# Loads of a turn released nine matmuls later, and one addition moved ahead of another in a two-layer kernel after retention

## The chip, the cores and the metric

The kernel runs on one core of a Trainium2 chip. The metric is the time of one execution on the device, in microseconds (us). The core has a matrix engine (PE, with its weight loads shown apart as PEld), a vector engine (DVE), a scalar engine (ACT), a general engine (POOL), and SP, which here issues nearly all DMAs. Each engine goes through its own list of instructions in order, and waits for others by semaphores.

## The reference

Eight batches, eight heads, 576 positions, head size 64. First retention, a causal attention without softmax whose scores decay by head; then a layer to 2048 and back to 512, with `h - tanh(h)` between:

```
scores = scale * np.matmul(q, k.transpose(0, 1, 3, 2))
gamma = 1.0 - 2.0 ** (-5.0 - np.arange(H))
Dmat = np.where(rel >= 0, gamma[:, None, None] ** rel[None, :, :], 0.0)
ret = np.matmul(scores * Dmat[None], v)          # (B, H, S, D)

x = ret.transpose(0, 2, 1, 3).reshape(B * S, H * D)   # 4608 x 512
h = x @ w_in                                     # 4608 x 2048
g = h - np.tanh(h)
out = g @ w_out                                  # 4608 x 512
```

## The kernel before, in words

**Tiling.** The 576 positions are cut into nine chunks of 64 (`n` or `c`, 0 to 8). A chunk of all eight batches is 512 tokens. The layer of 2048 is cut into 16 slices of 128 (`f`). Retention is done in chunks: a pair of batches (a *turn*, `m`) needs a tile of q and k (`qk`, 512 KB), a tile of v and k by rows (`vr`, 512 KB), and a running `state`. Matmuls take fp32 numbers split into a high and a low word, so a product of the two layers is three matmuls.

**Stages.** From chunk 2 on the program alternates between two kinds of stage. `stage_b(n)` does the second layer of chunk n and, beside it, retention of later chunks. Then `stage_a(na)` does the first layer of two chunks at once (na and na + 1), and the second layer of chunk na. The order is b(2), a(3), b(4), a(5), b(6), a(7), b(8).

**stage_b.** It has 16 steps, one for each slice f. An even step begins with `attend(m)`, the retention of one pair of batches: on PE 128 small matmuls (64x64 on quarters of the array). Each step has the 12 matmuls of `mm2(n, f)`; they need the two words of h of this slice (`gh` and `gl`, or `gs`), which `split` made two steps earlier out of a tile `s` that `fetch` brought back from DRAM (256 KB, it had been spilled there), four steps ahead. An even and the odd step after it make a turn. In the even step the program then issues `load_turn(..., 0, ...)`, the `qk` tile of three turns on, and the fetch of slice f + 4; in the odd step `load_turn(..., 1, ...)`, the `vr` tile of two turns on, and the next fetch. All four are on SP, in this order, and each `load_turn` is held back by `behind(tc, late)`: it waits until a named matmul of the step's own `mm2` is done (`names[2]` in even steps, `names[6]` in odd ones, counted from 0). What SP has behind it waits too.

In b(2) SP also gets the weights of the next stage (`ws`, `load_slot`: the first slot in quarters in steps 10 to 13, two slots of 1 MB in steps 14 and 15), the table of `work`, and at its end eight stores of the output (`out`, from the tiles `ob`).

**stage_a.** The first layer of two slices (a *pair* j of slices) by two chunks is done with seven products instead of eight (`product(0)` to `product(6)`, six matmuls each), whose results are combined on DVE: `u2` and `u4` are partial sums in the tile `work`, and `c22`, `c12`, x and `c21` are the four blocks of h. ACT and POOL or DVE make `h - tanh(h)` of them; `c22` and `c12` are spilled to DRAM for the next stage_b, the other two are split (`split`) and used at once by `mm2_pair`. In PSUM the products have five banks: x in `new` (for the first pair `o0`), y in `own`, z and v in two banks `h` that take turns. The work of the last block (`rest`: tanh, subtract, split of c21) follows directly in every pair but the first; the first pair's is put off into the second pair, ahead of `product(3)` and `c22`, by the list `pending`.

**What sets the order.** The order on every engine is the order in which the program is written (`in_order`); a tile's buffer is waited for where it is written next.

Of the kernel before, what the change touches and what calls it, by code (L numbers as in the profile page):

```python
# [14 lines left out]
ALU = mybir.AluOpType  # L15
# [50 lines left out]
def behind(tc, name):  # L66

    tc.add_manual_dep(
        tc.nc.cur_bb.bb.instructions[-1], name,
        mybir.DependencyInfo(mybir.DependencyClass.Sync, mybir.DependencyReason.DATA), reason="paced",  # L70
    )
# [3 lines left out]
def retention_ffn(ctx: ExitStack, tc: tile.TileContext, ins, out, spill, wvar):  # L75
    nc = tc.nc
# [120 lines left out]
    def load_qtab(c):  # L197
        if c not in qtabs:
            if c == 1:
                qtabs[c] = const.tile([P, 4, C], F32, tag="wo6", name="qtab1")  # L200
            else:
                qtabs[c] = pool.tile([P, 4, C], F32, tag="qtab", bufs=1, name=f"qtab{c}")
            nc.sync.dma_start(qtabs[c], qtab_d[c - 1])
# [495 lines left out]
    def place_of(f):  # L699
        return place("i", f) if f != 1 else "wi14"  # L700
# [85 lines left out]
    def load_turn(m, t, late=None):  # L786
        if m >= len(turns):
            return
        j = turns[m]
        c, b = divmod(j, B)  # L790
        if m == 1 and t == 0:
            load_qtab(c)
        if t == 0 and m and m % 8 == 0:
            tables.append(c)
        if t == 0 and m % 3 == 2:
            part = const.tile([P, 2, 2, 4, C], F32, tag=place_of(0), name=f"qk{j}")
        elif t == 0:
            part = pool.tile([P, 2, 2, 4, C], F32, tag="qk", bufs=2, name=f"qk{j}")
        else:
            part = pool.tile([P, 2, 2, 4, C], F32, tag=("vr", "one")[m % 2], bufs=1, name=f"vr{j}")  # L800
        nc.sync.dma_start(part, qkv_d[c - 1, ORDER[c].index(b) // 2, t])
        if late is not None:
            behind(tc, late)
        parts[j, t] = part
        for u in range(2):
            loaded.setdefault(j + u, Parts([None, None])).parts[t] = part[:, u]
# [92 lines left out]
    def load_slot(n, part=None):  # L899

        if n >= per * ((NC - FIRST) // 2):
            return
        if n not in slots:
            slots[n] = pool.tile([P, 4, 2, 2, P], F32R, tag=("xh0", "xh1", "xl0")[n % 3], bufs=1, name=f"ws{n}")
        at = slice(0, 4) if part is None else slice(part, part + 1)
        to = slots[n].bitcast(F32).rearrange("p v s c m -> p v (s c m)")[:, at]
        nc.sync.dma_start(to, wvar[:, 4 * (n % per) + at.start : 4 * (n % per) + at.stop])
# [3 lines left out]
    def product(v, into, start=True):  # L911

        n, at = divmod(count[0], 4)
        w, (xh, xl) = slots[n][:, at], xv[v]
        terms = [(a, x, k) for a, x in ((0, xh), (0, xl), (1, xh)) for k in range(2)]
        for i, (a, x, k) in enumerate(terms):
            nc.tensor.matmul(  # L917
                into, w[:, a, k], x[:, k], start=start and i == 0, stop=i == len(terms) - 1, skip_group_check=not start,
            )
        count[0] += 1  # L920
        if at == 3:
            load_slot(n + 3)

    def split(n, f, g, spare):

        if spare:
            both = const.tile([P, 2, BLK], F32R, tag=place_of(2), name="gs")
            gh, gl = both[:, 0], both[:, 1]
        else:
            gh = pool.tile([P, BLK], F32R, tag="gh", name=f"gh{n}_{f}")  # L930
            gl = pool.tile([P, BLK], F32R, tag="gl", name=f"gl{n}_{f}")
        nc.scalar.copy(gh, g)  # L932
        nc.vector.tensor_tensor(gl, g, gh.bitcast(F32), op=ALU.subtract)  # L933
        gs[n, f] = (gh, gl)

    def mm2_pair(n, j):

        if j == 0:
            ops[n] = [psp.tile([P, DM], F32, tag=f"o{t}", bufs=1, name=f"o{n}_{t}") for t in range(4)]
        fs, end = (2 * j + 1, 2 * j), j == NPAIR - 1  # L940
        if end:
            order = [(f, t, k) for t in range(4) for f in fs for k in range(3)]
        else:
            order = [(f, t, k) for f in fs for k in range(3) for t in range(4)]
        for f, t, k in order:
            g, a = [(gs[n, f][0], 0), (gs[n, f][0], 1), (gs[n, f][1], 0)][k]
            last_ = end and f == fs[1] and k == 2
            nc.tensor.matmul(  # L948
                ops[n][t], g[:, t * P : (t + 1) * P], wout[f][:, a, :],
                start=(j == 0 and f == fs[0] and k == 0), stop=last_,  # L950
            )
            if last_:
                store(n, t)

    def stage_a(na):

        nb, pending = na + 1, []
        u2, u4 = work[:, 0], work[:, 1]
        for j in range(NPAIR):
            x, y = [psp.tile([P, BLK], F32, tag=t, bufs=1, name=f"p{t}{na}_{j}") for t in ("new" if j else "o0", "own")]  # L960
            z, v = [psp.tile([P, BLK], F32, tag="h", bufs=2, name=f"p{t}{na}_{j}") for t in "zv"]
            f1, f2 = 2 * j, 2 * j + 1
            c22, c12, c21 = [pool.tile([P, BLK], F32, tag="g", bufs=3, name=f"c{t}_{na}_{j}") for t in (22, 12, 21)]

            def tanh(c):
                th = pool.tile([P, BLK], F32, tag="cv", bufs=4, name=f"th{na}_{j}")
                nc.scalar.activation(th, c, AF.Tanh)  # L967
                return th

            def away(c, f):  # L970
                nc.gpsimd.tensor_tensor(c, c, tanh(c), op=ALU.subtract)  # L971
                nc.sync.dma_start(spill[nb, f], c)

            product(0, x)
            product(1, y)
            nc.scalar.copy(u2, x)
            nc.vector.tensor_tensor(u2, y, u2, op=ALU.add)  # L977
            product(2, z)
            nc.vector.tensor_tensor(u4, z, u2, op=ALU.add)
            while pending:  # L980
                pending.pop()()
            product(3, v)
            nc.vector.tensor_tensor(c22, v, u4, op=ALU.add)  # L983
            y = psp.tile([P, BLK], F32, tag="own", bufs=1, name=f"py{na}_{j}")
            product(4, y)
            away(c22, f2)
            nc.vector.tensor_tensor(c12, y, u4, op=ALU.add)
            product(5, x, False)
            away(c12, f1)
            g11 = tanh(x)  # L990
            nc.vector.tensor_tensor(g11, x, g11, op=ALU.subtract)
            product(6, v, False)
            split(na, f1, g11, False)
            nc.vector.tensor_tensor(c21, v, u2, op=ALU.add)

            def rest(f=f2, c=c21, tanh=tanh):
                nc.vector.tensor_tensor(c, c, tanh(c), op=ALU.subtract)
                split(na, f, c, True)

            if j == 0:  # L1000
                pending.append(rest)
            else:
                mm2_pair(na, j - 1)
                rest()
        for f in range(3):
            fetch(nb, f)
        mm2_pair(na, NPAIR - 1)
        for f in range(2):
            split(nb, f, fetched.pop((nb, f)), False)
# [5 lines left out]
    def stage_b(n, m0):  # L1015

        fetch(n, 3)
        for f in range(NF):
            def ahead():
                if f + 2 < NF:  # L1020
                    split(n, f + 2, fetched.pop((n, f + 2)), f % 3 == 0)

            if n == 2 and f == 1:
                load_tables(FIRST)
            m, odd = m0 + f // 2, f % 2 == 1
            if n < NC - 1 and not odd:
                attend(m, ahead)
            else:
                ahead()
            if n == NC - 1:  # L1030
                fetch_on(n, f + 4)
            if n == 2 and f == NF - 1:
                load_slot(2)
            if (n, f) != (NC - 1, NF - 2):
                names = mm2(n, f)
            if n < NC - 1:
                load_turn(m + 3 - odd, int(odd), names[6 if odd else 2])
                fetch_on(n, f + 4)
            if odd and tables:
                load_tables(tables.pop())  # L1040
                set_tables()
            if n == 2 and f == 2:
                set_tables()
            if n == 2 and 9 < f < 15:
                load_slot(*((0, f - 10) if f < 14 else (1,)))
# [23 lines left out]
    work = pool.tile([P, 4, DM], F32, tag="xl1", bufs=1, name="work")  # L1069
# [63 lines left out]
```

## Time and profile before

| | |
|---|---|
| time, median of 3 | 859.01 us (855.62 to 859.25) |
| the profiled execution | 856.53 us, its span 854.8 us |
| PE busy in the span | 843.2 us (99%) |
| DVE, ACT, POOL busy | 484.6, 364.4, 74.3 us |
| DMA | 174.67 MB, 204 GB/s over the span |
| granted TensorE clock | 1.000 |

The span is the time from the first to the last instruction; some 1.7 us lie around it. PE is busy nearly all the time, so only the short stretches in which it waits are worth anything to a change that leaves PE's own work alone. The first 20 us and the last 5 us (start and end of the program) hold most of them.

### The profile page before, as it was taken

The numbers are of one execution on the slowest core, as the hardware profiler recorded it, in microseconds if no ns is written. First come the engines' busy times: TensorE is split into PE (matmuls) and PEld (weight loads), VectorE is DVE, ScalarE is ACT, GpSimd is POOL, SyncE is SP. The second block draws the span as 40 slices with busy tenths as digits, with TensorE's granted clock in tenths as the row PEclk, the third lists the DMA queues.
The fourth block names the chain that finished last, engine by engine and source line by source line (L and its number), as shares of the span: only waits on it lengthen the run. The fifth ranks groups of instructions, "written<-read, shape, count | busy, mean of one in ns | idle before, by whom it ended". The sixth has DMA issues, their size and how long they took to land.

```text
span 854.8 us, 18569 instructions
## 1 busy us (share of the span) xinstructions
PE 843.2 (99%) x7701; PEld 695.2 (81%) x7702; DVE 484.6 (57%) x817; ACT 364.4 (43%) x723; POOL 74.3 (9%) x63
## 2 busy tenths in 40 slices
PE   7999999999999999999999999999999999999998
PEld 6888888887888787888888788888888888888886
DVE  5989877868567665434346754434456554343321
ACT  4887774444234553323244443322345433232321
POOL 0001001110000001212110002211100012121100
PEclk9999999999999999999999999999999999999999
DMA  9976968776777579435376665534666255352432
GB/s 340 364 244 205 365 222 277 239 235 202 234 259 289 188 252 326 163 130 190 123 235 213 205 184 199 182 132 173 208 207 215 90 184 185 128 192 74 138 109 74
DMA packets 62404, 174.67 MB, mean 204 GB/s; under 512 B 7536, under 2 KB 8944, under 8 KB 57072
## 3 DMA queue, kind: packets, MB, share of 16 engines
q1 hardware_dynamic: 61792, 172.57, 59.5%
q8 instruction: 60, 0.98, 0.5%
q10 hardware_dynamic: 528, 0.92, 0.3%
q14 instruction: 24, 0.20, 0.1%
HBM read 124.70 MB, written 48.76 MB: 203 GB/s over the span
## 4 chain that ended last, share of the span: by engine, by line
PE 87%; issue 4%; DMA 4%; DVE 2%; ACT 1%; SPq 0%; POOL 0%; DVEq 0%; POOLq 0%; ACTq 0%
PE o L503 25%; PE o L948 15%; PE h L447 15%; PE pv L917 7%; PE pnew L917 6%; PE py L917 4%; PE pz L917 4%; PE pown L917 4%; PE s L300 3%; DMA s<-spill_dram 2%; PE new L300 2%; PE own L300 2%; DMA a<-in_first_dram 1%; PE po L917 1%; DMA rwi<-in_w_in_dram 1%
## 5 line engine op out<-in xcount | busy, mean ns | idle before, releaser
L503 PE MATMUL o<-wo,gh 128*128 128x512 f32 x608 | 156.8, 395 | 0.3 <-ACT gh L484 0.3
L503 PEld LDWEIGHTS o<-wo,gh 128*128 128x128 f32 x608 | 111.8, 188 | 26.8 <-ACT gh L484 2.2
L971 POOL TENSOR_TENSOR c<-c,th 128x512 f32<-128x512 f32 x48 | 62.0, 1297 | 516.6 <-ACT th L967 515.5
L967 ACT ACTIVATE th<-c 128x512 f32<-128x512 f32 x72 | 45.5, 632 | 140.9 <-DVE c L983 89.7
L447 PE MATMUL h<-xh,wi 128*128 128x512 f32 x384 | 97.7, 392 | 0.8 <-ACT xh L326 0.5
L447 PEld LDWEIGHTS h<-xh,wi 128*128 128x128 f32 x384 | 71.3, 188 | 16.9 <-ACT wi L129 0.8
L503 PE MATMUL o<-wo,gl 128*128 128x512 f32 x304 | 84.2, 389 | 0.0
L948 PE MATMUL o<-wo,gs 128*128 128x512 f32 x288 | 70.7, 389 | 0.0
L503 PEld LDWEIGHTS o<-wo,gl 128*128 128x128 f32 x304 | 57.1, 188 | 11.9
L948 PEld LDWEIGHTS o<-wo,gs 128*128 128x128 f32 x288 | 54.1, 188 | 11.2
L917 PE MATMUL pv<-xhv,ws 128*128 128x512 f32 x192 | 59.2, 390 | 0.6 <-DVE c L983 0.6
L503 PE MATMUL o<-wo,gs 128*128 128x512 f32 x240 | 59.2, 394 | 0.0
L300 PE MATMUL own<-qk,state 64*64 64x64 f32 x928 | 57.1, 221 | 0.0
L300 PE MATMUL own<-qk,vr 64*64 64x64 f32 x928 | 56.1, 218 | 0.7 <-issue 0.7
L977 DVE TENSOR_TENSOR work<-pown,work 128x512 f32<-128x512 f32 x24 | 16.6, 692 | 67.8 <-PE pown L917 67.1
L503 PEld LDWEIGHTS o<-wo,gs 128*128 128x128 f32 x240 | 44.4, 188 | 9.5
L917 PE MATMUL pnew<-xhv,ws 128*128 128x512 f32 x168 | 51.7, 389 | 0.0
L447 PE MATMUL h<-xl,wi 128*128 128x512 f32 x192 | 51.6, 389 | 0.0
L948 PE MATMUL o<-wo,gh 128*128 128x512 f32 x192 | 48.9, 389 | 0.0
L300 PEld LDWEIGHTS own<-qk,vr 64*64 64x64 f32 x928 | 46.6, 135 | 0.1
L300 PEld LDWEIGHTS own<-qk,state 64*64 64x64 f32 x928 | 46.2, 134 | 0.4 <-issue 0.4
L933 DVE TENSOR_TENSOR gl<-s,gh 128x512 fp32r<-128x512 f32 x44 | 30.0, 688 | 23.9 <-ACT gh L932 12.1
(152 smaller groups left out, 1516.4 us busy)
## 6 DMA issues: line engine op xcount, KB each, us to landing
ws<-wvar_dram SPq DMA_DIRECT2D x41, 1024.0 KB, 4.7
s<-spill_dram SPq DMA_DIRECT2D x94, 256.0 KB, 3.8
qk<-in_qkv_dram SPq DMA_DIRECT2D x29, 512.0 KB, 4.2
vr<-in_qkv_dram SPq DMA_DIRECT2D x29, 512.0 KB, 3.9
spill_dram<-c SPq DMA_DIRECT2D x48, 256.0 KB, 2.3
spill_dram<-g SPq DMA_DIRECT2D x36, 256.0 KB, 3.5
rwi<-in_w_in_dram SPq DMA_DIRECT2D x16, 512.0 KB, 5.6
rwo<-in_w_out_dram SPq DMA_DIRECT2D x16, 512.0 KB, 5.5
```

Source lines behind the costliest of these rows:

```text
L300: nc.tensor.matmul(out_, w, x, start=start, stop=stop)
L447: nc.tensor.matmul(hp, win[f][:, cc // 2, a, cc % 2 * P : (cc % 2 + 1) * P], x[:, cc, :], start=(k == 0), stop=(k == 3 * NCC - 1))
L503: nc.tensor.matmul(ops[n][t], g[:, t * P : (t + 1) * P], wout[f_][:, a, :], start=(f_ == first and k == 0), stop=(f_ == final and k == 2),)
L917: nc.tensor.matmul(into, w[:, a, k], x[:, k], start=start and i == 0, stop=i == len(terms) - 1, skip_group_check=not start,)
L933: nc.vector.tensor_tensor(gl, g, gh.bitcast(F32), op=ALU.subtract)
L948: nc.tensor.matmul(ops[n][t], g[:, t * P : (t + 1) * P], wout[f][:, a, :], start=(j == 0 and f == fs[0] and k == 0), stop=last_,)
L967: nc.scalar.activation(th, c, AF.Tanh)
L971: nc.gpsimd.tensor_tensor(c, c, tanh(c), op=ALU.subtract)
L977: nc.vector.tensor_tensor(u2, y, u2, op=ALU.add)
```

## The change

Three things. (1) In even steps of stage_b the `qk` load waits for the last matmul of the step (`names[11]`) and no longer for the third (`names[2]`); the fetch of h behind it on SP comes later with it. (2) In stage_a, `product(3)` and `c22` are written ahead of the put-off rest of the first pair. This matters in the second pair alone, where the list is not empty. (3) `u2` takes turns between two quarters of `work` (0 and 3), where it had one.

```diff
     def stage_a(na):
 
         nb, pending = na + 1, []
-        u2, u4 = work[:, 0], work[:, 1]
+        u4 = work[:, 1]
         for j in range(NPAIR):
+            u2 = work[:, 3 * (j % 2)]
...
             product(2, z)
             nc.vector.tensor_tensor(u4, z, u2, op=ALU.add)
+            product(3, v)
+            nc.vector.tensor_tensor(c22, v, u4, op=ALU.add)
             while pending:
                 pending.pop()()
-            product(3, v)
-            nc.vector.tensor_tensor(c22, v, u4, op=ALU.add)
             y = psp.tile([P, BLK], F32, tag="own", bufs=1, name=f"py{na}_{j}")
             product(4, y)
             away(c22, f2)
@@ stage_b
             if n < NC - 1:
-                load_turn(m + 3 - odd, int(odd), names[6 if odd else 2])
+                load_turn(m + 3 - odd, int(odd), names[6 if odd else 11])
                 fetch_on(n, f + 4)
```

**On DVE**, in the first stage_a (na = 3), from the last sum of the first pair (`c_3_0_4089` is its c21, `pv_1` and `py_1` are products of the second pair, `c_3_1_4160` its c22, `c_3_1_4161` its c12). Before:

```order
L994 TENSOR_TENSOR c_3_0_4089<-pv_0_4086,work 128x512 [waits PE_49]
L977 TENSOR_TENSOR work<-pown_1_4157,work 128x512 [waits PE_49,Activation_49]
L979 TENSOR_TENSOR work<-pz_1_4158,work 128x512 [waits DVE_49,PE_49]
L997 TENSOR_TENSOR c_3_0_4089<-c_3_0_4089,th_1_4186 128x512 [waits Activation_49]
L933 TENSOR_TENSOR gs<-c_3_0_4089,gs 128x512 [waits Activation_49]
L983 TENSOR_TENSOR c_3_1_4160<-pv_1_4159,work 128x512 [waits DVE_49,PE_49]
L987 TENSOR_TENSOR c_3_1_4161<-py_1_4199,work 128x512 [waits DMAHW5_49,PE_49,Pool_49]
```

With the change:

```order
L995 TENSOR_TENSOR c_3_0_4089<-pv_0_4086,work 128x512 [waits PE_49]
L978 TENSOR_TENSOR work<-pown_1_4157,work 128x512 [waits PE_49,Activation_49]
L980 TENSOR_TENSOR work<-pz_1_4158,work 128x512 [waits DVE_49,PE_49]
L982 TENSOR_TENSOR c_3_1_4160<-pv_1_4159,work 128x512 [waits DVE_49,DMAHW5_49,PE_49,Pool_49]
L998 TENSOR_TENSOR c_3_0_4089<-c_3_0_4089,th_1_4193 128x512 [waits Activation_49]
L933 TENSOR_TENSOR gs<-c_3_0_4089,gs 128x512 [waits Activation_49]
L988 TENSOR_TENSOR c_3_1_4161<-py_1_4199,work 128x512 [waits DMAHW6_49,PE_49,Pool_49]
```

The addition for c22 has moved ahead of two operations of the first pair, and it has new waits: it now takes the buffer of the first pair's c22, so it waits for POOL and for the store of that tile (`DMAHW5`), for which c12 waited before.

**On ACT**, in the same place. Before, and then with the change:

```order
L932 CAST gh_0_4151<-th_0_4142 128x512 [waits DVE_49]
L976 COPY work<-pnew_1_4156 128x512 [waits DVE_49,PE_49]
L967 ACTIVATE th_1_4186<-c_3_0_4089 128x512 [waits Pool_49]
L932 CAST gs<-c_3_0_4089 128x512 [waits DVE_49]
L967 ACTIVATE th_1_4208<-c_3_1_4160 128x512 [waits DMAHW7_49,DMAHW0_49,DVE_49]
```

```order
L932 CAST gh_0_4151<-th_0_4142 128x512 [waits DVE_49]
L977 COPY work<-pnew_1_4156 128x512 [waits PE_49]
L968 ACTIVATE th_1_4193<-c_3_0_4089 128x512 [waits DVE_49,Pool_49]
L932 CAST gs<-c_3_0_4089 128x512 [waits DVE_49]
L968 ACTIVATE th_1_4208<-c_3_1_4160 128x512 [waits DMAHW7_49,DMAHW0_49]
```

The order is as it was; the copy that begins u2 no longer waits for DVE, which is done with the last u2 only after c21.

**On SP**, at the end of b(2), where the rows read alike before and with the change (`qk_4047` is the load of step 14, the two `ws` behind it the 1 MB slots, `ob_0` the first tile of output, `vr_4081` the load of step 15, `c_3_0_4087` the first pair's c22):

```order
L801 DMA qk_4047<-in_qkv_dram 128x1024 [waits DMAHW0_49,DVE_49,PE_49]
L907 DMA ws_4049<-wvar_dram 128x2048 [waits DMAHW1_49]
L907 DMA ws_4051<-wvar_dram 128x2048 [waits DMAHW2_49]
L527 DMA out_dram<-ob_0_4056 64x512 [waits DMAHW3_49,Activation_49]
L527 DMA out_dram<-ob_0_4056 64x512 [waits DMAHW4_49]
...
L801 DMA vr_4081<-in_qkv_dram 128x1024 [waits DMAHW3_49,PE_49]
L907 DMA ws_4117<-wvar_dram 128x2048 [waits DMAHW4_49,PE_49]
```

Nothing moves in this list; the count of PE for which the first row waits is the one that lies nine matmuls later, and all that stands behind the row waits with it.

## The prediction

> **What bounds the kernel now.** I began with the page's first part, and then asked the busy times of the stages that the change touches (stretch, its length, busy us and count of PE, PEld, DVE, ACT, POOL; clock; DMA share; GB/s):
>
> ```profile
> PE 843.2 (99%) x7701; PEld 695.2 (81%) x7702; DVE 484.6 (57%) x817; ACT 364.4 (43%) x723; POOL 74.3 (9%) x63
> 262.00:303.00 41.00, 40.51 (x783) 33.53 (x772) 26.72 (x54) 20.17 (x53) 0.00 (x0) 1.00 0.65 227
> 303.00:341.00 38.00, 37.45 (x401) 30.61 (x400) 23.46 (x45) 16.07 (x39) 2.59 (x2) 1.00 0.86 294
> 443.00:506.00 63.00, 62.32 (x1221) 51.89 (x1221) 42.81 (x87) 31.89 (x85) 0.00 (x0) 1.00 0.62 198
> ```
>
> PE is the bound. Its holes are 0.49 us in b(2), 0.55 around the first stage_a, 0.68 in b(4). The change adds no matmul and takes none away, so it can win these holes and little more. Where they are is told by the chain of work that ended last (start, length, what): the 24 second-layer matmuls of a turn in b(2), b(4) and b(6), and a batch of 24 in stage_a.
>
> ```profile
> 277.58 5.67 PE o L503 x24
> 285.28 5.67 PE o L503 x24
> 293.69 4.55 PE o L503 x19
> 357.33 5.44 PE o L948 x24
> 475.81 5.67 PE o L503 x24
> 484.41 5.66 PE o L503 x24
> 634.86 5.67 PE o L503 x24
> 642.78 5.66 PE o L503 x24
> ```
>
> A turn takes 285.28 - 277.58 = 7.70 us. Three turns take longer: 293.69 - 285.28 = 8.41, 484.41 - 475.81 = 8.60, 642.78 - 634.86 = 7.92. Above 7.70 that is 0.71 + 0.90 + 0.22 = 1.83 us, one loss in each stage_b. PE's timeline shows the first two (in brackets the idle time and what ended it):
>
> ```profile
> 293.11 0.27 PE L300 MATMUL new<-vr 64*64 64x64 f32 x2 [0.49 <-issue]
> 483.94 0.21 PE L300 MATMUL own<-qk,vr 64*64 64x64 f32 x1 [0.68 <-issue]
> ```
>
> They lie inside `attend`, and no engine and no load ended them ("issue"). A turn has 152 matmuls (128 and 24) and as many weight loads, 304 instructions, and 256 of them pass in attend, in 7.70 - 5.67 = 2.03 us. So I looked for the queue of the instructions, q8, among the DMA queues (packets, MB, share). From 284.2 to 290.4 us and from 475.2 to 481.4 it moved nothing, while the loads' queue moved this:
>
> ```profile
> q1 hardware_dynamic: 510, 1.30, 60.9%
> q1 hardware_dynamic: 470, 1.15, 56.2%
> ```
>
> From 290.4 to 290.6 us its packet then started (the other one from 481.4 to 481.6):
>
> ```profile
> q8 instruction: 1, 0.02, 38.4%
> ```
>
> SP's issues of that turn, and the time in which its qk landed:
>
> ```profile
> 286.20 0.33 SPq L801 DMA_DIRECT2D qk<-in_qkv_dram  x1
> 289.84 0.33 SPq L801 DMA_DIRECT2D vr<-in_qkv_dram  x1
> qk<-in_qkv_dram SPq DMA_DIRECT2D x1, 512.0 KB, 3.5
> ```
>
> The packet started 0.7 us after qk had landed (286.20 + 3.5 = 289.7), and PE stood until 293.11. So these stops are, as I read them, PE without instructions, because the packet with them stood behind a burst of qk and h.
>
> The hole near 340 is another matter, and the chain tells it:
>
> ```profile
> 334.99 0.69 DVE c L994
> 335.76 0.59 ACT work L976
> 337.18 0.69 DVE work L979
> 339.15 0.70 DVE gs L933
> 339.95 0.70 DVE c L983
> 340.69 1.66 PE pv L917 x6
> ```
>
> PE's seventh product of the second pair (pv) waits for c22 (L983). On DVE that stands behind the put-off rest (which ends with L933), and u2's copy (L976) stands behind c21 (L994).
>
> **The change part by part.** *c22 and u2 (parts 2 and 3).* A matmul takes 5.44/24 = 0.227 us, a product of six 1.36. The pair's fourth product began at 335.87 (row below), so the seventh was due three products later, at 339.95, and began at 340.69; the hole costs 0.74. With c22 ahead of the rest, it needs only u4 (L979, ends at 337.87) and its product (335.87 + 1.36 = 337.23), and ends at 338.6, in time. Gain: 0.74. Late next is the rest, by the 0.7 us of one addition; its `gs` is used in the second half of the 24 matmuls that follow, 12 x 0.227 = 2.7 us behind the seventh product, which covers it; without that cover it would cost the 0.7. The new wait of c22, for the store of the first pair's c22, is the bound on the other side:
>
> ```profile
> 331.84 2.36 SPq L972 DMA_DIRECT2D spill_dram<-c  x2
> spill_dram<-c SPq DMA_DIRECT2D x1, 256.0 KB, 6.1
> ```
>
> The store lands at 331.84 + 6.1 = 337.9, so c22 ends at 338.6 all the same, before 339.95. Nothing, then.
>
> *The release (part 1) at the end of b(2).* Nine matmuls more are 9 x 0.227 = 2.04 us. On SP, behind the waiting qk, are two slots of weights and the eight stores; ACT waits for the stores, since its tanh takes over a buffer of `ob`:
>
> ```profile
> 317.69 0.33 SPq L801 DMA_DIRECT2D qk<-in_qkv_dram  x1
> 318.07 1.19 SPq L907 DMA_DIRECT2D ws<-wvar_dram  x2
> 321.16 8.34 SPq L527 DMA_DIRECT2D out_dram<-ob  x8
> 329.82 0.63 ACT L967 ACTIVATE th<-c 128x512 f32<-128x512 f32 x1 [5.40 <-DMA out_dram<-ob]
> 335.87 0.62 PE L917 MATMUL pv<-xhv,ws 128*128 128x512 f32 x2
> 317.50:318.50 1.00, 1.00 (x6) 0.83 (x5) 1.00 (x3) 0.78 (x3) 0.00 (x0) 1.00 0.00 0
> 318.50:329.50 11.00, 11.00 (x50) 9.12 (x49) 6.93 (x15) 3.76 (x10) 0.00 (x0) 1.00 0.92 312
> ```
>
> From 317.5 to 318.5 the DMA engines have nothing; from 318.5 they are 92% full for 11 us, until the stores have landed and ACT can begin. This heap starts with qk, so all of it comes 2.04 later: ACT's tanh at 331.86, and with it c21 (L994), which ends at 334.99 + 0.69 + 2.04 = 337.72. The fourth product of the second pair writes the bank that c21 reads, so PE, due there at 335.87, stands for 1.85 us. The seventh product is then due at 341.8, and c22 (its store lands 2.04 later too, at 340.0) ends at 340.7, in time. Net: +1.85 - 0.74 = +1.11. Bounds: -0.74 if the heap is no later, and +1.85 if c22's old hole comes back behind the new one. I take +1.11, since the empty stretch leaves the heap no earlier start.
>
> *The release in the turns: the data.* qk and h start 2.04 later, vr and the next h as before. The two bursts, now 289.84 - 286.20 = 3.64 us apart, come 1.6 apart and join. The first turn of b(6) has them so already, since SP was late there:
>
> ```profile
> 629.89 0.38 SPq L801 DMA_DIRECT2D qk<-in_qkv_dram  x1
> 631.73 0.33 SPq L801 DMA_DIRECT2D vr<-in_qkv_dram  x1
> qk<-in_qkv_dram SPq DMA_DIRECT2D x1, 512.0 KB, 4.2
> ```
>
> qk then lands 4.2 us after its issue, not 3.5. Its tightest use:
>
> ```profile
> 270.82 0.33 SPq L801 DMA_DIRECT2D qk<-in_qkv_dram  x1
> 278.23 0.68 DVE L255 TENSOR_TENSOR qk<-qk,work 128x512 f32<-128x512 f32 x1
> ```
>
> 270.82 + 2.04 + 4.2 = 277.1, still 1.1 before DVE takes it up, and PE needs what DVE makes of it only in the next attend (285.28 - 2.03 = 283.25), over 4 us on. So nothing; if that cover were gone, a miss of 1.5 us in one turn of each stage would cost 4.5, the bound from above. An earlier end has no way in here.
>
> *The release in the turns: the instructions.* This is the larger term, and the one least known. The DMA engines become free for 2 us more behind attend, where the packets of the three bad turns were asked for, so those get through. But the place at which a packet is asked for slides by 304 - 256 = 48 instructions a turn, so in each stage another one is asked for ahead of the joined burst, 2.04 us later in its turn. With only qk and h ahead of it, it loses what it loses now, 0.61 a stage (1.83/3). With vr and the next h ahead as well it waits for 768 KB more, 2.5 us at the 312 GB/s above, and loses 3.1. I take 1.05, much nearer the first, because vr is issued 1.6 us after qk, probably after the request; what it is above 0.61 stands for the 0.7 by which loads in a joined burst land later. Three stages: 3.15 - 1.83 = +1.3. Bounds: -1.83 (no stop left) and 9.3 - 1.83 = +7.5.
>
> [...]
>
> **The sum.** +1.3 + 1.11 = +2.4 us, against the profiled execution 856.53 + 2.4 = 858.9. That execution lies low among the four shown (855.62, 856.53, 859.01, 859.25), whose middle is 857.8; I forecast 857.8 + 2.4 = 860.2, which is 1.2 above the median of 859.01.
>
> **The rivals.** *Instructions get ahead of the loads.* For it: the 2 us that come free just where the bad packets were asked for. Against it: what is asked for in a joined burst waits longer. The three stops go: 857.8 - 1.83 + 1.11 = 857.1, and 857.8 - 1.83 - 0.74 = 855.2 if the heap at the end of b(2) costs nothing either. PE has no further hole there to win.
>
> *The joined burst decides* (slower). A packet that is asked for just ahead of the load of qk stands behind all 1.5 MB, once in each stage. It decides from the point where vr is issued before the packet is served. For it: the packet at 290.4 waited for all that was ahead. Against it: vr comes 1.6 us behind. Time: 857.8 + 7.5 + 1.11 = 866.4.
>
> *Data come late* (slower). A turn that misses its qk by 1.5 us in each stage: 860.2 + 4.5 = 864.7. Against it are the 1.1 us before DVE and the 4 behind it.
>
> *The change doesn't do what it says.* SP might reach qk late anyway, as at 629.89, and the release then moves nothing. For it speaks that one turn; in the one at 286.20, and at 317.69, SP had been waiting. Then parts 2 and 3 alone: 857.8 - 0.74 = 857.1.
>
> **How the numbers follow.** My forecast has 0.48, instructions ahead 0.25, the joined burst 0.16, late data 0.07, no effect of the release 0.04. A measurement of this kernel tells about 0.5%, 4.3 us, from no change. The forecast, the first rival and the last lie within that, 0.77 together; 0.05 of it I give to faster, for a first rival at its best in times that spread over 3.6 us: same 0.72, faster 0.05, slower 0.23 (the two slower rivals). The range goes from the best case, 855.2, to just short of the slower rivals: 855.5 to 864.6; the forecast's own is 858 to 863.
>
> **What would show it.** PE's timeline in the first stage_a: no hole before the seventh product of the second pair (part 2), but one of some 1.85 us before the fourth, ended by c21 (L995); ACT's first tanh there at some 331.9, behind the store of the output. SP's issues in even steps: qk 2 us later after the attend, 1.6 before vr. The turns of b(2), b(4), b(6): stops with "issue", about one a stage, in other turns than those at 285, 476 and 635, of 0.5 to 2 us. If there are none, the reading of the joined bursts was wrong; stops of 3 us mean that the joined burst decides; PE waiting for DVE or ACT in attend means late data. A time below 855.5 or above 864.6 would make the prediction wrong.

## The result, and the profile after

The changed kernel takes 863.22 us (median of 11 executions, 859.08 to 866.75). The kernel before, run beside it on the same chip, takes 855.31 (11 executions, 854.44 to 859.25). The ratio is 1.0078, with a 95% interval of 1.0052 to 1.0103: slower by 0.8%. The time lies inside the predicted range and 3 us above the predicted 860.2. Against the kernel before the loss is 7.9 us, where I had forecast 2.4. The before of this comparison is also faster than the three times shown with the prediction, whose median was 859.01, and than the 857.8 on which the forecast was built.

The profiled execution of the changed kernel took 860.08 us (span 858.3), that of the kernel before 856.53. The first row is from the page's first part, the others are busy times by stage with the columns of the prediction's first fence:

```profile
PE 844.7 (98%) x7701; PEld 696.1 (81%) x7702; DVE 485.6 (57%) x817; ACT 364.8 (42%) x723; POOL 74.1 (9%) x63
262.00:303.00 41.00, 38.47 (x760) 31.53 (x759) 25.57 (x51) 18.17 (x48) 0.00 (x0) 1.00 0.64 211
303.00:341.00 38.00, 37.29 (x399) 30.50 (x400) 21.89 (x43) 16.55 (x40) 2.58 (x2) 1.00 0.83 280
443.00:506.00 63.00, 61.49 (x1216) 50.90 (x1215) 39.73 (x80) 30.86 (x81) 0.00 (x0) 1.00 0.60 194
```

PE's busy time is that of before, within 1.5 us. In b(2) the same stretch of time holds 2.0 us less of it (38.47, before 40.51), and in b(4) 0.8 us less (61.49, before 62.32). The chain of work that ended last shows the turns, as it did before:

```profile
276.80 5.67 PE o L503 x24
285.82 5.29 PE o L503 x22
295.23 5.69 PE o L503 x24
...
478.71 5.67 PE o L503 x24
488.14 5.71 PE o L503 x24
...
638.63 5.67 PE o L503 x24
646.32 5.67 PE o L503 x24
```

The row at 285.82 has 22 matmuls and not 24, since a stop lies between the second and the third matmul of that turn. From 276.80 to 295.23 there are two turns, 18.43 us, 3.03 above twice 7.70 (before: 0.71). In b(4), 488.14 - 478.71 = 9.43, which is 1.73 above 7.70 (before: 0.90). In b(6), 7.69: nothing (before: 0.22). PE's timeline shows where the time is lost, with the idle time and what ended it in brackets:

```profile
285.82 0.51 PE L503 MATMUL o<-wo,gh 128*128 128x512 f32 x1 [0.67 <-issue]
294.65 0.27 PE L300 MATMUL new<-vr 64*64 64x64 f32 x2 [1.86 <-issue]
338.54 0.74 PE L917 MATMUL pv<-xhv,ws 128*128 128x512 f32 x2 [0.59 <-DVE c L995]
342.23 0.70 PE L917 MATMUL pnew<-xhv,ws 128*128 128x512 f32 x2 [0.63 <-DMA ws<-wvar_dram]
487.67 0.21 PE L300 MATMUL own<-qk,vr 64*64 64x64 f32 x1 [1.50 <-issue]
```

By the starts of the matmuls around them, the two stops in b(2) cost 0.84 and 2.05 us, and the two in the first stage_a 0.75 and 0.79. The stops at 294.65 and 487.67 are at the same instructions as the stops of before at 293.11 and 483.94, and three times and twice as long; the one at 285.82 is new. All in all the profiled execution has 3.03 + 1.73 + 0.75 + 0.79 + 0.35 (a short wait near 316 for DVE's scaling of qk, L255, in a turn of 8.04 us) = 6.65 us of stops against 0.71 + 0.90 + 0.22 + 0.74 = 2.57 before. That is 4.1, where the two profiled executions differ by 860.08 - 856.53 = 3.55.

The issues of SP in a turn, then those at the end of b(2), with ACT's first tanh in the first stage_a and the busy times of the heap of transfers in between:

```profile
279.77 0.33 SPq L801 DMA_DIRECT2D qk<-in_qkv_dram  x1
281.36 0.33 SPq L801 DMA_DIRECT2D vr<-in_qkv_dram  x1
...
321.66 0.33 SPq L801 DMA_DIRECT2D qk<-in_qkv_dram  x1
332.63 0.63 ACT L968 ACTIVATE th<-c 128x512 f32<-128x512 f32 x1 [6.30 <-DMA out_dram<-ob]
322.50:333.00 10.50, 10.50 (x48) 8.70 (x47) 5.34 (x10) 2.04 (x5) 0.00 (x0) 1.00 0.97 336
```

qk and vr now come 1.6 us apart, as forecast. One thing the profiled execution does not show: the median execution is 3.1 us slower than it. The granted clock of the executions tells them apart. The four with a mean clock of 0.999 or 1.000 took 859.08 to 860.08. The seven with 0.993 to 0.998 took 861.48 to 866.75, and the two at 0.993 are the two slowest. More on this stands with the fourth and the fifth experiment.

### The profile page after: what moved, and what is told of

Read it like the earlier page. It is cut to its first block, busy times and chain, and to the rows that moved or that the text cites. A ratio compares the mean times of both kernels' runs of the same rounds, so it can differ in the third digit from the quotient of the medians.

```text
span 858.3 us, 18565 instructions
## 1 busy us (share of the span) xinstructions
PE 844.7 (98%) x7701; PEld 696.1 (81%) x7702; DVE 485.6 (57%) x817; ACT 364.8 (42%) x723; POOL 74.1 (9%) x63
## 4 chain that ended last, share of the span: by engine, by line
PE 90%; DMA 5%; DVE 2%; issue 1%; ACT 1%; SPq 0%; DVEq 0%; ACTq 0%
PE o L503 26%; PE o L948 15%; PE h L447 15%; PE pv L917 7%; PE pnew L917 7%; PE py L917 4%; PE pz L917 4%; PE pown L917 4%; PE s L300 3%; PE new L300 2%; PE own L300 2%; DMA s<-spill_dram 2%; DMA ws<-wvar_dram 1%; PE po L917 1%; DMA work<-in_qtab_dram 1%
```

## The experiments

The theory to be tested was the prediction's: PE's stops come from packets of instructions that stand behind loads, and the later release makes them stand there longer. Against it stood that late data, or the end of b(2), carry the loss.

**One part alone.** The first kernel makes part 1 only (the release), the second parts 2 and 3 only (c22 and u2).

```
-                load_turn(m + 3 - odd, int(odd), names[6 if odd else 2])
+                load_turn(m + 3 - odd, int(odd), names[6 if odd else 11])
```

> Part 1 alone on the kernel before. Theory (the release makes packets of instructions wait behind joined bursts, and delays the heap of loads and stores at the end of b(2)): the whole loss is here, 862.5 to 865, at least the 863.2 of the full change, with stops of 0.8 to 2 us ended by nothing but issue in b(2) and b(4). Rival (the loss comes from c22's new wait for a store, part 2): no loss, 855.3.

Measured: 861.49 us (857.86 to 863.27), ratio 1.006 [1.0036, 1.0083], 1 us below the expected range. PE has the stops of the changed kernel, and one in b(6) as well:

```profile
285.63 0.73 PE L503 MATMUL o<-wo,gh 128*128 128x512 f32 x2 [0.67 <-issue]
294.17 0.27 PE L300 MATMUL new<-vr 64*64 64x64 f32 x2 [1.58 <-issue]
487.11 0.21 PE L300 MATMUL own<-qk,vr 64*64 64x64 f32 x1 [1.78 <-issue]
647.28 0.33 PE L300 MATMUL own<-qk,vr 64*64 64x64 f32 x2 [1.53 <-issue]
```

The second kernel is the changed one with the old release:

```
-                load_turn(m + 3 - odd, int(odd), names[6 if odd else 11])
+                load_turn(m + 3 - odd, int(odd), names[6 if odd else 2])
```

> Parts 2 and 3 alone. Theory: the hole of 0.74 us before the seventh product of the second pair goes, the three stops in the turns stay as before, 854.6, ratio 0.999. Rival (c22 waits for the store of the first pair's c22 and holds DVE up): the hole stays or grows, 855.3 to 857.

Measured: 854.09 us (853.58 to 855.75, 11 executions), ratio 0.9976 [0.9967, 0.9985]. Its PE has no hole in the first stage_a, so c22 ahead of the rest wins the 0.74 of before. The measured gain is larger: 0.0024 of 856.30, 2.1 us, and 1.3 to 2.8 by the interval. The turns around the stops of b(2) and b(4):

```profile
284.34 5.67 PE o L503 x24
292.47 5.67 PE o L503 x24
...
473.70 5.67 PE o L503 x24
481.75 5.67 PE o L503 x24
```

They lose 8.13 - 7.70 = 0.43 and 8.05 - 7.70 = 0.35, where the kernel before lost 0.71 and 0.90 with the loads of these turns released alike. So a stop can differ by half a microsecond between two executions that load alike, and only one execution of each kernel is profiled; whether this part of the gain belongs to c22 and u2 is open. What follows: the release carries the whole loss, c22 and u2 are a small gain. This kernel is faster than both the kernel before and the changed one.

**The end of b(2) released as before.** The changed kernel, but step 14 of b(2) keeps the third matmul.

```
-names[6 if odd else 11]
+names[6 if odd else 2 if (n, f) == (2, NF - 2) else 11]
```

> The full change, but the qk load of step 14 of b(2) is released by the third matmul as before. Theory: the two stops of the first stage_a (0.75 and 0.79 us) go, the stops in the turns stay: 861 to 862.5. Rival (the heap at the end of b(2) is the main cost): 856 or less.

Measured: 861.35 us (857.07 to 863.92), ratio 1.0057 [1.0035, 1.0079]. The holes of the first stage_a are gone, the stops of the turns are not: 0.74 and 1.5 us in b(2), and 9.15 - 7.70 = 1.45 in b(4). So the turns carry most of the loss. Stage_a has about 1.5 us of it by the trace; the two ratios, 1.0057 and 1.0078, have intervals that overlap.

**vr later as well, so that the two bursts are apart again.**

```
-names[6 if odd else 11]
+names[11]
```

> The full change, and the vr load of odd steps also released by the last matmul, not the seventh, so that the two bursts of a turn are again 2.8 us apart and no longer join. Theory (packets of instructions wait for the joined burst): the stops shrink to those of before, 857 to 859.5. Rival (data come late, DVE and ACT wait for vr and qk): vr comes 1.1 us later still, so more is lost, 864 to 868.

Measured: 861.15 us (859.1 to 865.02), ratio 1.0063 [1.0037, 1.009]. The stops stay: 0.84 and 2.05 us in b(2), 1.45 in b(4). With that the joined burst is out as the cause: here vr is issued 2.7 us behind qk, and the packet waits all the same. In this turn qk and h alone are enough. Something else shows in this execution: behind the stop of 2.05 us, the 24 matmuls of the turn take longer. The chain, then the busy times of that stretch (the clock is the third number from the right):

```profile
296.17 7.29 PE o L503 x24
...
296.10:299.80 3.70, 3.70 (x15) 2.93 (x10) 2.65 (x5) 2.82 (x8) 0.00 (x0) 0.55 0.02 8
299.80:303.50 3.70, 3.70 (x21) 2.75 (x22) 0.69 (x1) 0.62 (x1) 0.00 (x0) 0.99 0.47 147
```

7.29 in place of 5.67: the granted clock is 0.55 for 3.7 us, and the stop costs 1.6 us more than its own length. The mean clock of the executions of this kernel goes with their time in the same way: 0.999 to 1.000 for 859.1 to 860.0, 0.994 and 0.995 for 864.7 and 865.0.

**Are the stops tied to the count of instructions?** The changed kernel with 24 small matmuls (48 instructions) ahead of b(2).

```
+    extra = psp.tile([P, BLK], F32, tag="new", bufs=1, name="extra")
+    for i in range(24):
+        nc.tensor.matmul(extra[:, :64], wout[i % NF][:, 0, :P], wout[i % NF][:, 0, :64], start=True, stop=True)
     stage_b(2, 0)
```

> The full change with 24 matmuls of 64 columns (24 weight loads with them, 48 instructions) that nobody reads, put on PE ahead of b(2). A turn has 304 instructions and a packet 256, so the places at which packets are needed move by 48 instructions, one turn. Theory (PE without instructions): the stops that were in the fourth and fifth turn of b(2) (0.84 and 2.05 us) and the sixth of b(4) (1.69) come one turn earlier, at the places 48 instructions ahead of those. Rival (data late, or something else tied to the turns): they stay in their turns. Time 1 to 2 us more for the added matmuls.

Measured: one execution, 868.6 us, 5.4 above the changed kernel's median where 1 to 2 was expected. The stops have moved one turn ahead (the first two below stand in the third and the fourth turn of b(2), where the changed kernel has them in the fourth and the fifth), and so has that of b(4); a new one has come at the end of b(2):

```profile
281.67 0.63 PE L503 MATMUL o<-wo,gh 128*128 128x512 f32 x2 [0.74 <-issue]
290.41 0.27 PE L300 MATMUL new<-vr 64*64 64x64 f32 x1 [2.04 <-issue]
327.40 0.96 PE L503 MATMUL o<-wo,gs 128*128 128x512 f32 x3 [2.26 <-issue]
```

48 instructions are 304 - 256, the step by which a packet's place slides in a turn. So the stops belong to a place in the stream of instructions, not to a load or an operand.

The traces of all thirteen kernels (before, changed and eleven experiments) say so more exactly. I count PE's matmuls, weight loads and its few (116) semaphore and drain instructions from the start of an execution. Then the stops of 0.4 us and more that end with "issue" in b(2), b(4) and b(6) come at 6336 and 10176 in the kernel before, at 6080, 6336 and 10176 in the changed kernel, and with 48 more instructions at 5824, 6080, 7360 and 9920. Each of these is 192 more than a multiple of 256, and in the other ten kernels it is 192 or 193. The queue q8 fits this: in the changed kernel, as in the one before, it moves 60 packets of 16 KB each, about one for every 256 of the 15403 matmuls and weight loads (15403/60 = 256.7).

```profile
q8 instruction: 60, 0.98, 0.4%
```

Two of the stops with 48 more instructions are longer than 2 us, and behind each of them seven or eight matmuls start 0.427 us apart and not 0.227 (1.6 us each, the same drop of the clock: 0.77 from 290.9 to 298.3 us and 0.78 from 327.4 to 330.0, where the fourth experiment has 0.77 from 296.1 to 303.5).

**When may qk be issued?** The next three kernels move the loads inside the turn. The first spreads them: qk by the third matmul, its h by the ninth, vr by the third matmul of the odd step.

```
-                load_turn(m + 3 - odd, int(odd), names[6 if odd else 11])
+                load_turn(m + 3 - odd, int(odd), names[2])
                 fetch_on(n, f + 4)
+                if f + 4 < NF:
+                    behind(tc, names[8])
```

> Parts 2 and 3, with the four loads of a turn spread out: qk and vr released by the third matmul of their steps, each fetch of h by the ninth of its own. Theory: a packet of instructions then stands behind 512 or 768 KB at most and mostly less, the stops in the turns shrink below those of before: 853 to 855, ratio 0.997 to 1. Rival (any delay of the fetch of h costs, data late): above 856.

Measured: 859.71 us (857.69 to 861.86), ratio 1.005 [1.0029, 1.007]. The expectation missed: the stops of b(2) are 0.57 and 2.05 us, that of b(4) 1.72, and b(6) has one of 1.76, although qk is as early as before.

> The full change, with qk released by the seventh matmul, between before's third and the change's last. Theory: the bursts are 2.7 us apart and just do not join, 855 to 859. Rival (every microsecond of delay costs alike): in the middle of the two, 859 to 860.

This one releases qk by the seventh matmul (names[6]). Measured: 856.42 us (855.45 to 857.91, 10 executions), ratio 1.0009 [0.9994, 1.0024]: no loss. The stops are 0.40 in b(2) and 0.35 in b(4), as small as with the old release; b(6) has one of 0.61, where the old release lost 0.2. The reason that I had given does not hold: in that turn of b(4) the two bursts do join (from 480.0 to 484.3 us the DMA engines never pause for 0.3 us).

The third fetches h at once and holds only qk for the last matmul.

```
-                load_turn(m + 3 - odd, int(odd), names[6 if odd else 11])
+                if odd:
+                    load_turn(m + 2, 1, names[6])
                 fetch_on(n, f + 4)
+                if not odd:
+                    load_turn(m + 3, 0, names[11])
```

> The full change, but the fetch of h in even steps stands ahead of the qk load on SP and so isn't held back; qk alone waits for the last matmul. Theory (size of the joined burst): the joined burst has 1.25 MB, not 1.5, so somewhat less is lost: 859 to 862.5. Rival (h comes late): all is won back, 855.

Measured: 859.47 us (858.97 to 866.78), ratio 1.0063 [1.0039, 1.0087]; 0.84 and 2.05 us in b(2), 0.90 in b(4). The time is in the expected range, but the longest stop has not shrunk with the burst.

Neither "qk late" nor "joined bursts" fits these. So I compared at what moment of its turn the packet starts for which PE stands (the trace has a packet's start, not when it was asked for), and formed a new theory: the packet is asked for so that it would start about 5.3 us behind the first of a turn's 24 second-layer matmuls, whatever the loads do, and if a transfer runs at that moment, it waits for the end of that. Three more kernels test that.

**Less behind qk.** The changed kernel, the h of the even step fetched with vr.

```
+                if odd and f + 3 < NF:
+                    fetch(n, f + 3)
+                    behind(tc, names[6])
                 load_turn(m + 3 - odd, int(odd), names[6 if odd else 11])
-                fetch_on(n, f + 4)
+                if odd:
+                    fetch_on(n, f + 4)
```

> The changed kernel, but the h of an even step is fetched in the odd step behind it, released by the same matmul as vr (the seventh), so that behind the last matmul of the even step only qk starts, 512 KB in place of 768. Counted from the first of a turn's 24 second-layer matmuls, the packet of instructions that PE waits for started at 5.3 us in the kernel before and in the kernel with the release at the seventh matmul, whether qk was issued at 1.0 or at 1.9, and at 6.6 to 6.9 in the changed kernel, just where the transfer of qk and h ended. Theory (the packet is asked for so that it would start at 5.3 and waits for whatever transfer covers that moment): qk alone ends near 5.8, so the packet starts at 5.6 to 6.0 and the stop in the fifth turn of the first stage_b is 0.6 to 1.0 us and not 2.05, that in its counterpart of the second stage_b 0.5 to 0.9 and not 1.69; time 857 to 860. Rival (what counts is that the load is issued late, not how long it runs): packet at 6.6 and stops of 1.7 to 2.1 as in the changed kernel, 860 to 863.

**A release in between**, by the ninth matmul (names[8]):

> The changed kernel with qk and h released by the ninth matmul of the even step, between the seventh (stops of 0.40 and 0.32 us) and the twelfth (2.05 and 1.69). Theory (the packet would start at 5.3 us and waits for the transfer that covers that moment): qk is issued at 2.4, the transfer ends near 6.0, the packet starts there, and the stops are 0.9 to 1.3 and 0.7 to 1.1; time 857 to 859. Rival (a threshold: the packet comes either before or after the whole pair): stops as at the seventh or as at the twelfth, nothing between.

**vr by the last matmul, qk by the third** (names[11 if odd else 2]), so that little should run near 5.3:

> c22 and u2 as in the changed kernel, qk and the h with it released by the third matmul as before, and vr and its h by the last matmul of the odd step in place of the seventh: the two transfers of a turn end near 4.5 and near 9, and nothing runs from 4.5 to 6.8 us of a turn. Theory (the small stops that are left do not come from waiting for a transfer, but from the time that a packet takes after it is asked for, and 5.3 us is the earliest start): packet at 5.3 again, stops of 0.2 to 0.5 in the same turns, 853 to 855.5, ratio 0.995 to 1.000 to the kernel before. Rival (the small stops are what is left of a wait for a transfer, as my prediction read them): with the second transfer gone from that place the packet starts earlier or runs faster and no stop is left, some 0.7 us less than with c22 and u2 alone. Second rival (vr comes too late for its scaling): ACT waits for vr by some 1 us a turn, PE stops in the next attend, 857 or more.

Measured, in that order: 859.64 us (855.88 to 862.17), ratio 1.0043 [1.0022, 1.0064]; 856.93 (855.13 to 860.32), ratio 1.0015 [0.9998, 1.0031]; 854.82 (852.91 to 858.51), ratio 0.9991 [0.997, 1.0012]. The first two stop for 0.95 us in the fifth turn of b(2), the third for 0.40; the theory had said 0.6 to 1.0, 0.9 to 1.3 and 0.2 to 0.5. Not all fits: the second is slightly faster than expected and has two stops more (0.57 in b(2), 0.65 in b(6)), and the third stops for 0.62 in b(4). The turn of b(4) in the chain, and the packet of instructions, queue q8, among the DMA queues. With h put off, the packet starts from 484.0 to 484.2 us:

```profile
478.33 5.67 PE o L503 x24
486.93 5.66 PE o L503 x24
...
q8 instruction: 1, 0.02, 30.8%
...
486.46 0.21 PE L300 MATMUL own<-qk,vr 64*64 64x64 f32 x1 [0.68 <-issue]
```

With the release at the ninth, from 484.9 to 485.1:

```profile
479.05 5.67 PE o L503 x24
487.65 5.67 PE o L503 x24
...
q8 instruction: 1, 0.02, 29.9%
...
487.19 0.21 PE L300 MATMUL own<-qk,vr 64*64 64x64 f32 x1 [0.68 <-issue]
```

With vr late, from 478.2 to 478.4, while the end of qk and h is still running on some DMA engines before it and nothing after (DMA share and GB/s are the last two columns):

```profile
473.06 5.67 PE o L503 x24
481.38 5.66 PE o L503 x24
...
477.50:478.20 0.70, 0.70 (x5) 0.58 (x4) 0.00 (x0) 0.00 (x0) 0.00 (x0) 1.00 0.24 94
478.40:479.50 1.10, 1.10 (x58) 0.84 (x60) 0.00 (x0) 0.00 (x0) 0.00 (x0) 1.00 0.00 0
```

So this kernel did not keep the moment free, as had been meant. With parts 2 and 3 alone it is free: the packet starts from 478.8 to 479.0, and nothing ran just before. In the changed kernel nothing runs earlier in the turn, from 2.7 to 3.9 us into it, and the packet does not start there. In this order:

```profile
478.52:478.90 0.38, 0.38 (x3) 0.33 (x2) 0.00 (x0) 0.00 (x0) 0.00 (x0) 1.00 0.00 0
481.45:482.60 1.15, 1.15 (x6) 0.95 (x6) 0.40 (x2) 1.15 (x5) 0.00 (x0) 1.00 0.00 0
```

In the changed kernel the packet starts from 485.4 to 485.6; from 479.8 to 485.4 only q1 moved anything:

```profile
q1 hardware_dynamic: 370, 1.02, 55.4%
```

The same turn of b(4) in all kernels but the one with 48 more instructions, in the order of the packet's start. The start is counted from the first of the turn's 24 matmuls; the stop is the turn's length in the chain less 7.70:

| kernel | qk and h released by matmul | packet starts, us into the turn | stop, us |
|---|---|---|---|
| parts 2 and 3 alone | third | 5.2 | 0.35 |
| vr by the last matmul | third | 5.3 | 0.62 |
| release by the seventh | seventh | 5.4 | 0.35 |
| h ahead of qk | twelfth, h at once | 5.6 | 0.90 |
| before | third | 5.7 | 0.90 |
| h put off to vr | twelfth, h later | 5.7 | 0.90 |
| release by the ninth | ninth | 5.9 | 0.90 |
| end of b(2) as before | twelfth | 6.4 | 1.45 |
| vr later as well | twelfth | 6.4 | 1.45 |
| spread | third, h by the ninth, vr early | 6.5 | 1.72 |
| changed kernel | twelfth | 6.7 | 1.73 |
| part 1 alone | twelfth | 6.8 | 2.00 |

Two things are constant in it. PE needs the packet 7.23 us into the turn: 487.67 - 1.73 - 478.71 in the changed kernel, 483.94 - 0.90 - 475.81 before, 486.46 - 0.90 - 478.33 with h put off, 487.19 - 0.90 - 479.05 (7.24) with the ninth. And PE goes on 2.2 to 2.5 us after the packet's start (487.67 - 485.4, 483.94 - 481.5, 486.46 - 484.0, 487.19 - 484.9). So the stop is about the start plus 2.3, less 7.23. A packet that starts at its earliest, 5.2 to 5.4, still costs 0.35 to 0.62. With parts 2 and 3 alone no transfer was in its way just then. But no run takes qk and h out of the microseconds ahead as well, so what sets this earliest start is open. In the kernel before, PE began the last 256 instructions ahead of the stop 1.9 us into the turn in b(4), and 0.3 us into it in b(2), and the packet started at 5.7 and 5.2. A packet that starts later than that makes the stop longer, microsecond for microsecond on the whole, though in steps (see the last section).

Each packet of q8 has 16 KB (60 of them are 0.98 MB), and the stops come 256 instructions apart or a multiple of that (6336 - 6080 = 256, 10176 - 6336 = 15 x 256). Counted as above, no packet in any of the thirteen kernels starts more than 298 instructions ahead of the place at which PE would stop for it, so a packet comes little more than its own 256 instructions ahead.

## Why the prediction was right and wrong

**What bounds the kernel, and what it can win.** Right. PE has the same work, and the stops account for the difference of the two profiled executions (4.1 us of stops, 3.55 us of time).

**c22 and u2 (parts 2 and 3).** Right. Alone they remove the hole of 0.74, and what comes late behind them costs nothing. That the kernel with them alone is faster by 2.1 us, and not by 0.74, I had not foreseen. In the changed kernel the hole before the seventh product is gone too.

**The release at the end of b(2): +1.85, less 0.74.** The place and the mechanism were right, the size was not. The hole before the fourth product is there, ended by c21 (L995), but costs 0.75. The heap starts later, but moves 336 GB/s and not 312, and is done sooner; ACT's tanh is 2.8 us later than before (332.63 for 329.82), while PE itself was by then 1.9 us later (the last turn of b(2) has its first second-layer matmul at 318.6, before at 316.7), so that only 0.9 of the 2.04 reached stage_a. Not foreseen was the next wait: a slot of weights, from the same heap, is late for the sixth product and costs 0.79. Together 1.54, near the 1.85 for reasons that only half agree.

**The release in the turns: the data.** Nearly right: I had put it at nothing, and 0.35 us near 316 is all that late data cost in the profiled execution.

**The release in the turns: the instructions, +1.3.** Here the prediction went wrong in its reading and too low in its size. The sign came out right. The term was 1.05 a stage, 3.15 in all; measured are 3.03, 1.73 and 0 in the profiled execution, 4.76 in all, and part 1 alone shows 1.72 in b(6) (by the starts of the matmuls around the stop at 647.28). Three steps of it fell:

- "The packet stood behind a burst of qk and h" is at most part of what made the stops of before. Released 0.9 us later, by the seventh matmul, the same burst moved the packet's start in b(4) by no more than 0.2 us (5.4, where parts 2 and 3 alone have 5.2), and the earliest start costs 0.35 even with the DMA engines empty. Of the 0.7 us between qk's landing and the packet's start, which I had taken for a trail of the burst, h has the first part: it was fetched behind qk, and its last packet ended at 290.2. From 290.25 to 290.50 nothing ran.
- "Those get through": I had expected the two free microseconds behind attend to let the packets of the three bad turns pass, and others to be caught. In b(6) of the changed kernel that is what happened: the packet started 1.4 us into the turn, between 639.9 and 640.1, ahead of qk, and there is no stop. In b(2) and b(4) the bad turns stayed bad. Their packets did not start in the free stretch (in b(4) 2.7 to 3.9 us into the turn), and the new place of qk and h lies just on the moment at which they start otherwise. The fourth turn of b(2) came on top, since the packet ahead is caught too.
- "The joined burst" adds nothing. The stops are the same with vr 2.7 us behind qk, and stops of 3 us did not come. (With the loads spread out, vr comes early and the packet starts at 6.5; by the order of the issues it is then vr that holds it.)

How sharp the edge is, the ratios tell: 1.0009 for a release by the seventh matmul, 1.0015 by the ninth, 1.0078 by the twelfth.

**A term that was missing: the clock.** Three stops, of 2.05, 2.2 and 2.4 us, were each followed by seven or eight matmuls at about half the clock (0.427 us apart in place of 0.227), at 1.6 us each. The profiled execution of the changed kernel had none, but its median execution has a mean clock of 0.997, which is 0.003 x 860 = 2.6 us, nearly all of the 3.1 by which it is slower than the profiled one. That the drops in those executions come behind these same stops was not shown, since only one execution of each kernel is profiled. In the profiled ones the three drops stand behind those stops, and three other stops of 2.05 had none. Drops come elsewhere too: in the kernels with h ahead of qk and with the release by the ninth matmul, the clock was 0.53 from 16.0 to 23.2 us and from 15.4 to 19.0, at the start of the program (their mean clocks are 0.996 and 0.998). The kernel before also has executions with a mean clock of 0.995 and 0.996, at 858.70 and 858.02 us.

**What the packet waits for.** The packet starts 5.4, 5.9 and 6.7 us into the turn with qk and h released by the seventh, the ninth and the twelfth matmul, and at 5.7 for the twelfth without h, 256 KB less. As I read it, it had waited for h as well as for qk.

**The rivals.** "Instructions get ahead of the loads" is true of b(6) in the changed kernel, and wrong for b(2) and b(4). "The change doesn't do what it says" is out. "The joined burst decides" and "data come late" named the right sign by the wrong mechanism.

**The luck in the number.** The loss was forecast 7.9 - 2.4 = 5.5 us too low. The kernel before was taken as 857.8 and measured 855.31, 2.5 too high, and that covers nearly half of it. So the time came out 3 us off, inside the range.

**Still open.** What sets the earliest start of a packet in b(2) and b(4), why the packet of b(6) starts earlier in some executions (no stop in the changed kernel, 1.7 us with part 1 alone), why the kernel before stops for 0.90 us in b(4) where parts 2 and 3 alone stop for 0.35, and what starts a drop of the clock.

## What to carry to other kernels

This program issues many short instructions in a burst (256 in 2.03 us) and was bound there by how instructions arrive; a load that was put into the gap ahead of the burst delayed them (stops of 2.05 and 1.73 us, before 0.71 and 0.90), however well it suited the data. Before a transfer is moved in a kernel with such bursts, look in the trace for the queue of the instructions, note when its packets start within a loop's turn, and keep that moment free; a release by the seventh matmul hardly moved the packet here (5.4) and cost nothing, one by the twelfth cost 0.6 to 0.8%. A kernel's own profile can be milder than its median: compare the granted clock over all executions, since a stop of 2 us was here sometimes paid nearly twice. And one profiled execution tells little about half a microsecond in a single stop.

## What the runs showed of the hardware that I had not expected

The lengths of these stops come in steps: 0.35, 0.62, 0.90, 1.45, 1.72 and 2.00 us in b(4), each 0.27 or 0.28 or twice that from the next, in kernels whose loads were moved by other amounts. I have no explanation for the step.

Behind three stops beyond 2 us (2.05, 2.2 and 2.4 us) the granted clock fell to about half: 0.55 over 3.7 us for the first of them, with 128x512 matmuls 0.427 us apart in place of 0.227. Seven or eight matmuls were so slow each time; eight of 0.427 are 3.4 us. A stop of 2.05 us inside a stretch of small matmuls was enough, though not each time: three others of 2.05 had no drop behind them.
